# The output product of an attention, SoLU and expert kernel moved one round further behind the hidden product, and the expert slots' row transposes issued ahead of their weight loads

## The chip, the cores and the metric

One core of a Trainium2 chip runs one launch. The metric is device time in microseconds (us); lower is better. The engines are TensorE (PE in the rows; PEld is its weight load), VectorE (DVE), ScalarE (ACT), GpSimd (POOL) and SyncE (SP), which issues most of the transfers. L516 is line 516 of the kernel.

## The reference

The inputs are attention tensors of 8 batches, 8 heads, 576 positions and 64 dimensions, and the weights of two layers behind it.

```python
# 1: attention inside chunks of 64 positions
scores = q_c @ k_c.T / 8;  attn = softmax(scores);  x = attn @ v_c      # -> 4608 tokens x 512
# 2: a SoLU layer
h = x @ w_in                                       # 4608 x 1024
solu = h * softmax(h)
ln = (solu - mean) / sqrt(var + 1e-6) * g_ln
x2 = ln @ w_out                                    # 4608 x 512
# 3: each token goes to the one expert with its largest logit
e = argmax(x2 @ w_gate);  gate = max of softmax(x2 @ w_gate)
out = gate * sigmoid(x2 @ w_output_gate)[e] * (relu(x2 @ w1[e]) @ w2[e])
```

All products run in float16 pairs (a high part and a rest), three matmuls for one.

## The kernel before, in words

**Stage 1** works on 36 tiles of 128 tokens (NT = 36). It is a software pipeline written out by hand: a table of step names, each with an offset. In round i the step `ma+0` handles tile i, `pv+1` tile i+1, and so on; each engine runs its own instructions in exactly this order. START (lines 38 to 47) lists the first rounds one by one, BODY (lines 50 to 53) the rest; the loop at line 825 runs BODY for rounds 4 to 37. The steps that matter here:

- `ma` (m1, L461): the hidden product h of a tile, 24 matmuls of 512 columns on PE into the one pair of PSUM banks of `ps_h`.
- `hm`, `eh`, `um` (L472 to L492): row maximum on DVE (L474), exponential on ACT (L481), their product u on DVE (L488), which is h's last reader. The next `ma` cannot start before it.
- `uh`, `ul`, `ud` (L507 to L522): u is centred and split, its high half on ACT (L510), its rest on DVE (L516), and `ud` has SP transpose both by a DMA (L521) into `uT`, of which there are three buffers.
- `mb` (m2, L524; in the loop through `m2_tile`, L791): the output product x2, 48 matmuls (L534), from `uT` into the one pair of PSUM banks of `ps_x`.
- `ev`, `el` (L540, L553): x2 is read out, on ACT (logits L548, rows L550) and on DVE (L556). The next `mb` cannot start before both.
- `ro`, `rk`, `pa` (L559, L586, L601): tokens are routed in groups of four tiles: `ro` some seven small DVE instructions and a few on POOL, `rk` two small matmuls, `pa` some eight more DVE instructions (L610 to L620). `send` (L770) then scatters a tile's rows to DRAM from POOL (L644).
- `pr`, `pe`, `pv`, `qk` and the steps around them: the attention of tiles one to three ahead. `ya`, `yb`: one expert weight piece is split on ACT (L273) and DVE (L274), in every third round two, until 40 of 64 are done.

Before the change `mb` handles tile i-1 and `ev`, `el`, `ro` tile i-2. The last tile's `m2_tile` puts the first expert slot's first product `ffn1(0)` ahead of m2(35) on PE. At the end of round 33 POOL also gathers the rows of three early slots (L182), which SP transposes in rounds 34 to 36 (L192).

**Stage 2** (from line 854) runs expert slots of 128 tokens. Slot s has on PE `ffn1` (tile hc, 96 matmuls; j = 0, 1) and `ffn2` (tile y, 24 matmuls), one slot after the other. Even slots use weight lane W0, odd ones W1. While slot s runs, SP issues for slot s+2: the first matrix (`wload(s+2, parts=[0])`, L950, two transfers of 1 MB, carried out only where the lane changes its expert), the transpose of the slot's gathered rows (`xtr_slot`, L192), the next weight piece's store and load, and, after `ffn2(s)`, the second matrix. The rows are gathered by POOL (L182) at the end of the slot before.

SP works strictly in order. The program's transfers from SP and ACT take turns on eight completion counters, and one waits until the transfer that had its counter before has landed, whether or not it needs that data. Which transfers fall on one counter follows from the order of the program.

Of the kernel before, what the change touches and what calls it, by code (L numbers as in the profile page):

```python
# [20 lines left out]
NT = NTOK // P  # L21
# [7 lines left out]
GRP = max(GROUPS)  # L29
# [7 lines left out]
FIRST = 4  # L37
# [4 lines left out]
gm1 oh5 tp3 su2 te3 wp0 gm2 no1V tp4 ld6 te4 ex2 gm3 hm0 tp5 pt1 te5 ph1 gm4 qk3 tp6 ol1 te6 ol7 gm5 eh0 tp7 ol6 te7  # L42
pl1 gm6 pv1 gm7 mx3 sm2 no2G xh1 su3 sc4G xl1 um0 ex3 pt2 ol5 oh4 uh0 ma1 hi4 ph2 sq0 sm3 ul0 ol3 sc6G pl2 lo4G ol0
ol4 ol2 pv2 hm1 xh2 ld7 gE0 eh1 no3G xl2 qk4 mb0 mx4 pt3 su4 hi5 sc7A um1 ph3 ss0 ex4 uh1 lo5V qk5 ld8 ev0 pl3 sm4
no4G pv3 ma2 ul1 sq1 mx5 el0 xh3 xl3 su5 hi6 pt4 mb1 lo6G qk6 ex5 ph4 hm2 eh2 pl4 sc8A sm5 um2 ss1 pv4 uh2 ev1 ma3
no5G sq2 xh4 hi7 ul2 mx6 ld9 xl4 pt5 su6 ex6 el1 sm6 mb2 hm3 no6G ph5 eh3 pl5 um3 ss2 sq3 uh3 ul3 lo7G ss3
"""


BODY = """  # L50
ev-2 el-2 pe+1 ph+2 pl+2 ya+0 ys+0 yl+0 ma+0 yb+0 yt+0 ym+0 pv+1 qk+3 hq+4 hk+4 xh+1 lq+4 sA+0 lk+4 sB+0 hm+0
eh+0 xl+1 sc+5 mx+3 um+0 uh+0 su+3 ex+3 sq+0 ul+0 mb-1 sm+3 ud+0 pr+2 rk-3 pa-3 ld+6 no+3 ss+0 ro-2
"""


# [10 lines left out]
def tile_attention_solu_moe(  # L66
# [12 lines left out]
    V, A, G, T, SP = nc.vector, nc.scalar, nc.gpsimd, nc.tensor, nc.sync  # L79
# [14 lines left out]
    spare = const.tile([P, 1], F32, name="spare")  # L94
# [81 lines left out]
    def sync(i, o):  # L176
        tc.add_manual_dep(i.ins, o.ins.name, mybir.DependencyInfo(
            mybir.DependencyClass.Sync, mybir.DependencyReason.DATA), reason="order")

    def gather(s, gx, far, after=()):  # L180
        x = xs[s % NX]
        i = G.indirect_dma_start(out=x.bitcast(I32), out_offset=None, in_=rows,  # L182
                                 in_offset=bass.IndirectOffsetOnAxis(ap=gx, axis=0),
                                 bounds_check=NE * NTOK - 1, oob_is_err=False)
        for o in after:
            sync(i, o)
        cst["x", s] = (x, far)
        cst["g", s] = i

    def xtr(s, xT):  # L190
        x, _ = cst["x", s]
        SP.dma_start_transpose(out=xT.rearrange("p s k t -> p (s k) t"), in_=x[:, 0:DM].bitcast(F16))  # L192
        cst["xT", s] = xT
# [45 lines left out]
    def reach(s):  # L239

        order = range(NE) if s % 2 == 0 else range(NE - 1, -1, -1)
        n = sum(s // 2 >= k for k in FILL[s % 2])
        return set(order) if n == 3 else set(order[:n + 1])
# [43 lines left out]
    with ExitStack() as ab:  # L287
# [225 lines left out]
        def ulo(t):  # L513
            u, se, _ = st["u", t]
            us = st["us", t]
            V.scalar_tensor_tensor(out=us[:, 1], in0=u, scalar=se[:, 2:3], in1=us[:, 0], op0=ALU.add, op1=ALU.subtract)  # L516

        def u_tr(t):
            us = st.pop(("us", t))
            uT = u_p.tile([P, 2, FC, P], F16, tag="uT", name="uT", bufs=3)  # L520
            SP.dma_start_transpose(out=uT.rearrange("p s f t -> p (s f) t"), in_=us.rearrange("p s f -> p (s f)"))  # L521
            st["uT", t] = uT  # L522
# [221 lines left out]
        def consts(_):  # L744
# [8 lines left out]
            ld=load, sc=scale_qv, hi=split_hi, lo=split_lo, qk=qk, mx=smax, su=ssub, ex=sexp, sm=ssum, no=snorm,  # L753
            pt=pt_pe, ph=pt_hi, pl=pt_lo, pv=pv, xh=xt_hi, xl=xt_lo, ma=m1, hm=hmax, eh=exph, um=umul, uh=uhi,
            sq=stats, ul=lambda t: (ulo(t), u_tr(t)), ss=stats2, mb=m2, ev=x2_ev, el=x2_lo,
# [14 lines left out]
        def send():  # L770
            nonlocal sent
            if sent < routed:
                scatter(sent)
                sent += 1
# [39 lines left out]
        def early_pieces(t, n, f):  # L814
            if t < NT - 2 and done[0] < AHEAD and (n == 0 or t % 3 == 1):
                f()

        steps.update(
            ph=p_hi, pl=p_lo, pr=p_tr, pe=pt_ev, ul=ulo, ud=u_tr, hq=qv_hi, hk=k_hi,
            lq=qv_lo, lk=k_lo, mb=m2_tile, rk=rank, pa=place_rows,  # L820
            ro=route_rows, sA=lambda t: ok(t + 4) and send(), sB=lambda t: ok(t + 4) and send(),
            ya=lambda t: early_pieces(t, 0, piece_split), ys=lambda t: early_pieces(t, 0, piece_store),
            yl=lambda t: early_pieces(t, 0, piece_load), yb=lambda t: early_pieces(t, 1, piece_split),
            yt=lambda t: early_pieces(t, 1, piece_store), ym=lambda t: early_pieces(t, 1, piece_load))
        for i in range(FIRST, NT + 2):
            if i - FIRST < NX:
                G.memset(xs[i - FIRST], 0.0)
            for name in BODY.split():
                t = i + int(name[2:])
                if ok(t):  # L830
                    steps[name[:2]](t)
            if not ok(i + 4):
                n = 2 if i < NT else GRP
                while n and sent < routed:
                    send()
                    n -= 1
                    if n:
                        G.memset(spare, 0.0)
            if i == NT - 3:
                raws = [raw_p.tile([P, 3, 512], F32, tag="raw", name=f"raw{j}") for j in range(2)]  # L840
                for j in range(EARLY):
                    gather(j, egx[:, j:j + 1], efar[:, j:j + 1],
                           after=[scattered[t] for t in range(sum(GROUPS[:EG + 1]))])
                    G.memset(spare, 0.0)
            if NT - 2 <= i < NT - 2 + EARLY:
                j = i - (NT - 2)
                xtr(j, raws[0][:, j].bitcast(F16).rearrange("p (s k t) -> p s k t", s=2, k=KC))
            for n in range(2):
                if 0 <= i - (NT - 5) < 4:
                    m, kc = divmod(2 * (i - (NT - 5)) + n, KC)  # L850
                    SP.dma_start(out=W0[m][:, kc], in_=(wsp1, wsp2)[m][0, :, kc])


    with ExitStack() as cs:
# [50 lines left out]
        def new(tag, k):  # L905
            return x_p.tile([P, 2, 4, P], F16, tag=tag, name=tag, bufs=k)
# [30 lines left out]
        def wload(s, e=None, parts=(0, 1)):  # L937
            kw = {}
            if e is None:
                if 0 in parts:  # L940
                    cst["e", s] = (SP.value_load(ei[0:1, s:s + 1], min_val=0, max_val=NE - 1),
                                   SP.value_load(ei[0:1, NS + s:NS + s + 1], min_val=0, max_val=1))
                e, c = cst["e", s]
                kw = dict(cond=(c > 0))
            for m in parts:
                for hk in range(2):
                    kk = slice(2 * hk, 2 * hk + 2)
                    src = (wsp1, wsp2)[m]
                    src = src[e, :, kk] if not kw else src[ds(e, 1), :, kk].rearrange("a p k s f -> (a p) k s f")
                    i = SP.dma_start(out=W[s % 2][m][:, kk], in_=src, **kw)  # L950
                    can = reach(s) if kw else {e}
                    assert not can & {x for _, x, _ in pieces[done[0]:]}, (s, can, done)
                    for o, x in stores:
                        if x not in can:
                            tc.declare_no_dep(i.ins, o.ins, reason="another expert")
                    wloads.append((i, can))
                    if not kw:
                        sync(i, (scattered[-1], cst.get(("g", EARLY + 1)))[m])

        def next_piece():  # L960
            piece_split()
            piece_store()
            piece_load()

        def fetch_slot(k):
            gather(k + EARLY, gx[:, k:k + 1], far[:, k:k + 1], after=scattered if k == 0 else ())

        def xtr_slot(k):
            xtr(k + EARLY, new("xT", 3))

        def ffn(s, w, between=lambda: None):
            ffn1(s, w[0], [new("hT0", 2), new("hT1", 2)])
            between()
            ffn2(s, w[1])
# [15 lines left out]
        def slots(a, b):  # L990
            for s in range(a, b):
                def between():
                    if s + 2 < b:
                        wload(s + 2, parts=[0])
                        xtr_slot(s + 2)
                        next_piece()

                ffn(s + EARLY, W[s % 2], between)
                if s + 2 < b:
                    wload(s + 2, parts=[1])  # L1000
                    if s % 8 == 7:
                        next_piece()
                put(s + EARLY, x_p)
                if s + 3 < b:
                    fetch_slot(s + 3)
                else:
                    G.memset(spare, 0.0)

        slots(0, OFTEN)
        n = nc.values_load(ei[0:1, 2 * NS:2 * NS + 1], min_val=0, max_val=NS)  # L1010
# [63 lines left out]
```

## Time and profile before

| | |
|---|---|
| median of 3 runs | 988.37 us (985.55 to 988.44) |
| the profiled execution | 986.18 us, of which its span is 984.2 us |
| granted TensorE clock, mean | 0.974 |
| stage 1, first to last x2 matmul | 94 to 547 us |
| stage 2, first to last slot | 576 to 979 us |
| DMA, mean over the span | 204 GB/s |

The profile lists for each engine its instructions with start, duration, and the idle time ahead of them with what ended it. A row of the timeline reads: start in us from the span's start, duration in us, engine, line, operation, tile written <- tiles read, shapes, count; in brackets the idle time before it and the releaser. A row of the waits reads: who waited <- for whom: us in total, times, longest. A row of the chain of waits gives start, duration and the piece of work; "DMA" there is the time from issue to landing. Ends of matmuls are modelled, so steps on PE are best read from start to start.

### The profile page before, as it was taken

To read this page: it belongs to the slowest core of one execution; us is meant where nothing else is said; L and a number is where in the kernel's file an instruction comes from. 1 tells how busy PE (TensorE), PEld (TensorE's weight loads), DVE (VectorE), ACT (ScalarE), POOL (GpSimd) and SP (SyncE) were. 2 spreads that over 40 slices of the span, in tenths; PEclk is the share of its full clock that TensorE was granted. 3 is DMA by queue.
4 is the path that set the end of the run, shared out by engine and by line. 5 is a ranking of instruction groups with operands and counts; after the bars stand their busy time and mean duration, and the time that the engine had idled before them with its cause. 6 is when DMAs were issued, how large, how long until landed. Compare 5 with 4: busy or idle time off the path is not lost.

```text
span 984.2 us, 26880 instructions
## 1 busy us (share of the span) xinstructions
PE 897.7 (91%) x11230; PEld 635.1 (65%) x11230; DVE 538.3 (55%) x964; ACT 453.6 (46%) x697; POOL 402.9 (41%) x503
## 2 busy tenths in 40 slices
PE   0378999998999899989999999998999999999996
PEld 0165666666666666656667767775776677777774
DVE  7947679898988888888875613221222222111110
ACT  3435677776777777777663123232222222111111
POOL 4815366767666766666534321121111121121120
PEclk9956999999999999999999999999999999999999
DMA  9432467877786978778678677889799753943252
GB/s 381 144 107 55 106 175 208 241 229 228 230 262 194 276 222 237 234 196 254 183 226 202 167 231 230 269 246 287 204 265 309 231 172 101 339 128 78 65 172 92
DMA packets 161442, 201.18 MB, mean 204 GB/s; under 512 B 123164, under 2 KB 123164, under 8 KB 156192
## 3 DMA queue, kind: packets, MB, share of 16 engines
q1 hardware_dynamic: 148576, 158.39, 56.7%
q0 software_dynamic: 9280, 28.40, 8.5%
q10 hardware_dynamic: 3456, 12.58, 3.5%
q8 instruction: 90, 1.47, 0.6%
q14 instruction: 40, 0.33, 0.1%
HBM read 244.40 MB, written 53.51 MB: 303 GB/s over the span
## 4 chain that ended last, share of the span: by engine, by line
PE 46%; DVE 28%; DMA 8%; issue 8%; ACT 6%; POOL 2%; SPq 2%; DVEq 0%; ACTq 0%; POOLq 0%
PE hc L92 19%; PE y L92 16%; DVE us L516 5%; PE x L534 5%; DVE ws L274 4%; DVE u L488 4%; ACT us L510 3%; DVE mm L474 3%; PE h L92 3%; DMA uT<-us 2%; DMA xT<-xs 2%; DMA w<-wsp 2%; DVE ssum L376 2%; PE gx L736 1%; ACT ws L273 1%
## 5 line engine op out<-in xcount | busy, mean ns | idle before, releaser
L92 PEld LDWEIGHTS <-w 128*128 128x128 f16 x3840 | 220.6, 99 | 17.5 <-issue 7.2
L534 PE MATMUL x<-wo,uT 128*128 128x272 f16 x1728 | 204.3, 279 | 18.9 <-DMA uT<-us 16.2
L206 DVE SCALAR_TENSOR_TENSOR hT<-hc,hT 128x512 f16<-128x512 f32 x78 | 53.9, 691 | 295.5 <-ACT hT L205 289.2
L92 PE MATMUL hc<-xT,w 128*128 128x128 f16 x3552 | 207.7, 220 | 5.0 <-DMA xT<-xs 5.0
L92 PE MATMUL y<-w,hT 128*128 128x512 f16 x936 | 208.9, 379 | 1.7 <-DMA w<-wsp 1.5
L92 PE MATMUL h<-wi,xT 128*128 128x512 f16 x864 | 196.1, 384 | 10.5 <-DVE xT L456 8.6
L534 PEld LDWEIGHTS <-uT 128*128 128x128 f16 x1728 | 167.6, 99 | 48.2 <-DMA uT<-us 18.5
L226 POOL DMA_INDIRECT out_dram<-o,ix x40 | 40.8, 1021 | 326.8 <-ACT o L225 306.8
L92 PEld LDWEIGHTS <-hT 128*128 128x128 f16 x936 | 89.7, 98 | 103.6 <-issue 2.1
L92 PEld LDWEIGHTS <-xT 128*128 128x128 f16 x864 | 83.6, 99 | 107.4 <-DVE xT L456 9.5
L205 ACT ACTIVATE hT<-hc 128x512 f16<-128x512 f32 x78 | 46.6, 597 | 155.5 <-PE hc L92 147.2
L324 POOL TENSOR_TENSOR qv<-raw,qv 128x1024 f16<-128x1024 f32 x35 | 81.3, 2322 | 44.7 <-ACT qv L315 44.7
L225 ACT ACTIVATE o<-y,xs 128x512 f32<-128x512 f32 x40 | 27.5, 688 | 152.2 <-PE y L92 141.5
L274 DVE SCALAR_TENSOR_TENSOR ws<-wf,ws 128x1024 f16<-128x1024 f32 x64 | 79.4, 1253 | 31.6 <-ACT ws L273 31.4
L383 POOL TENSOR_TENSOR p<-p,ssum 128x512 f32<-128x512 f32 x35 | 38.1, 1088 | 134.9 <-DVE ssum L378 71.0
L273 ACT ACTIVATE ws<-wf 128x1024 f16<-128x1024 f32 x64 | 65.9, 1044 | 22.2 <-DMA wf<-in_w_dram 20.6
L516 DVE SCALAR_TENSOR_TENSOR us<-u,se,us 128x1024 f16<-128x1024 f32 x36 | 61.1, 1696 | 23.4 <-ACT us L510 23.2
L510 ACT ACTIVATE us<-u,se 128x1024 f16<-128x1024 f32 x36 | 41.3, 1148 | 49.3 <-DVE se L490 49.3
L481 ACT ACTIVATE e<-h,mm 128x1024 f32<-128x1024 f32 x36 | 40.1, 1114 | 37.5 <-DVE mm L475 37.5
L488 DVE SCALAR_TENSOR_TENSOR u<-h,e 128x1024 f32<-128x1024 f32 x36 | 44.0, 1223 | 7.2 <-ACT e L481 3.2
L474 DVE TENSOR_REDUCE mm<-h 128x1 f32<-128x1024 f32 x36 | 43.8, 1217 | 6.3 <-PE h L92 6.3
L644 POOL DMA_INDIRECT rows<-row,ix x36 | 39.1, 1086 | 16.1 <-DVE row L620 8.0
(183 smaller groups left out, 972.3 us busy)
## 6 DMA issues: line engine op xcount, KB each, us to landing
w<-wsp SPq DMA_DIRECT2D x152, 1024.0 KB
wf<-in_w_dram SPq DMA_DIRECT2D x64, 512.0 KB
raw<-in_qvk_dram SPq DMA_DIRECT2D x36, 768.0 KB
wsp<-ws SPq DMA_DIRECT2D x40, 512.0 KB
wsp<-ws ACTq DMA_DIRECT2D x24, 512.0 KB
w<-in_w_in_dram SPq DMA_DIRECT2D x4, 1024.0 KB
w<-wsp SPq DMA_DIRECT2D x8, 512.0 KB
wo<-in_w_out_dram SPq DMA_DIRECT2D x2, 1024.0 KB
```

The source lines that it names most:

```text
L92: T.matmul(ps, lhsT=l, rhs=r, start=(i == 0), stop=(i == n - 1))
L205: A.activation(t[:, 0], h, AF.Relu)
L206: V.scalar_tensor_tensor(out=t[:, 1], in0=h, scalar=0.0, in1=t[:, 0], op0=ALU.max, op1=ALU.subtract)
L226: i = G.indirect_dma_start(out=out, out_offset=bass.IndirectOffsetOnAxis(ap=ix, axis=0), in_=o, in_offset=None, bounds_check=NTOK - 1, oob ...
L273: A.activation(s16[:, 0], f, AF.Copy, scale=S_E)
L274: V.scalar_tensor_tensor(out=s16[:, 1], in0=f, scalar=S_E, in1=s16[:, 0], op0=ALU.mult, op1=ALU.subtract)
L324: E.tensor_tensor(out=qv[:, 1], in0=raw, in1=qv[:, 0], op=ALU.subtract)
L474: V.tensor_reduce(mm[:, 0:1], h.rearrange("p a b -> p (a b)"), axis=AX.X, op=ALU.max)
L488: V.scalar_tensor_tensor(out=u, in0=h.rearrange("p a b -> p (a b)"), scalar=S_U / (S_X * S_WI), in1=e, op0=ALU.mult, op1=ALU.mult, accum_o ...
L510: A.activation(us[:, 0], u, AF.Identity, bias=se[:, 2:3])
L516: V.scalar_tensor_tensor(out=us[:, 1], in0=u, scalar=se[:, 2:3], in1=us[:, 0], op0=ALU.add, op1=ALU.subtract)
L534: T.matmul(x2[:, z, 0:n], lhsT=uT[:, a, f], rhs=wo[b][:, f, z, 0:n], start=(f + a + b == 0), stop=(last and a + b == 0))
```

## The change

The three later steps (`ev`, `el`, `mb`) and the routing that follows are moved one round further back: `mb` from tile i-1 to i-2, `ev`, `el` and `ro` from i-2 to i-3, `rk` and `pa` from i-3 to i-4. START gives up one `mb`, one `ev` and one `el`; the loop gets one more round, 38. The scatters at the end have a small POOL memset behind each instead of between them, and the round from which four may be sent is one later. In stage 2 the transpose of slot s+2 is issued ahead of the first matrix of slot s+2 instead of behind it.

```diff
-no4G pv3 ma2 ul1 sq1 mx5 el0 ... sc8A sm5 um2 ss1 pv4 uh2 ev1 ma3
-no5G sq2 xh4 hi7 ul2 mx6 ld9 xl4 pt5 su6 ex6 el1 sm6 mb2 hm3 no6G ...
+no4G pv3 ma2 ul1 sq1 mx5 el0 ... sc8A sm5 um2 ss1 pv4 uh2 ma3
+no5G sq2 xh4 hi7 ul2 mx6 ld9 xl4 pt5 su6 ex6 sm6 hm3 no6G ...
 BODY = """
-ev-2 el-2 pe+1 ph+2 pl+2 ya+0 ys+0 yl+0 ma+0 ...
-eh+0 xl+1 sc+5 ... ul+0 mb-1 sm+3 ud+0 pr+2 rk-3 pa-3 ld+6 no+3 ss+0 ro-2
+ev-3 el-3 pe+1 ph+2 pl+2 ya+0 ys+0 yl+0 ma+0 ...
+eh+0 xl+1 sc+5 ... ul+0 mb-2 sm+3 ud+0 pr+2 rk-4 pa-4 ld+6 no+3 ss+0 ro-3
...
-        for i in range(FIRST, NT + 2):
+        for i in range(FIRST, NT + 3):
...
-                n = 2 if i < NT else GRP
+                n = 2 if i <= NT else GRP
                 while n and sent < routed:
                     send()
                     n -= 1
-                    if n:
-                        G.memset(spare, 0.0)
+                    G.memset(spare, 0.0)
...
                     if s + 2 < b:
+                        xtr_slot(s + 2)
                         wload(s + 2, parts=[0])
-                        xtr_slot(s + 2)
                         next_piece()
```

## Rows read from the trace of the kernel before

**Rows 1.** The profile's busy time, share of the span and instructions of each engine:

```profile
PE 897.7 (91%) x11230; PEld 635.1 (65%) x11230; DVE 538.3 (55%) x964; ACT 453.6 (46%) x697; POOL 402.9 (41%) x503
```

**Rows 2.** Waits of the whole execution: PE for the transposed u, and in stage 2:

```profile
PE x L534 <- DMA uT<-us: 16.2, 14, 3.0
...
PE hc L92 <- DMA xT<-xs: 5.0, 2, 4.1
```

**Rows 3.** Waits of DVE alone, 127 to 512 us:

```profile
DVE us L516 <- ACT us L510: 19.8, 31, 2.4
...
DVE mm L474 <- PE h L92: 0.8, 2, 0.4
```

**Rows 4.** Timeline, DVE: the row maximum of tile 6 and of tile 32:

```profile
157.31 1.21 DVE L474 TENSOR_REDUCE mm<-h 128x1 f32<-128x1024 f32 x1
...
494.67 1.22 DVE L474 TENSOR_REDUCE mm<-h 128x1 f32<-128x1024 f32 x1
```

**Rows 5.** Timeline, PE: h of two tiles, with no wait between them:

```profile
139.74 5.34 PE L92 MATMUL h<-wi,xT 128*128 128x512 f16 x24
...
151.80 5.34 PE L92 MATMUL h<-wi,xT 128*128 128x512 f16 x24
```

**Rows 6.** Timeline, PE: end of stage 1, h of tiles 33 to 35 and what follows:

```profile
499.88 5.34 PE L92 MATMUL h<-wi,xT 128*128 128x512 f16 x24
...
512.10 5.34 PE L92 MATMUL h<-wi,xT 128*128 128x512 f16 x24
...
524.75 5.34 PE L92 MATMUL h<-wi,xT 128*128 128x512 f16 x24
530.38 5.57 PE L534 MATMUL x<-wo,uT 128*128 128x272 f16 x48 [0.29 <-DMA uT<-us]
535.79 4.68 PE L92 MATMUL hc<-raw,w 128*128 128x128 f16 x81
...
541.72 4.89 PE L534 MATMUL x<-wo,uT 128*128 128x272 f16 x42
...
547.17 5.34 PE L92 MATMUL y<-w,raw 128*128 128x512 f16 x24
```

**Rows 7.** Timeline, DVE, end of stage 1: u of tile 32, the last rounds' chain, the readout:

```profile
497.40 1.23 DVE L488 SCALAR_TENSOR_TENSOR u<-h,e 128x1024 f32<-128x1024 f32 x1
...
525.87 0.18 DVE L610 TENSOR_TENSOR rw<-rt,eoff 128x32 f32<-128x32 f32 x1
...
527.20 0.72 DVE L556 SCALAR_TENSOR_TENSOR row<-x,se,row 128x512 f16<-128x512 f32 x1
...
530.13 1.23 DVE L474 TENSOR_REDUCE mm<-h 128x1 f32<-128x1024 f32 x1 [2.21 <-PE h L92]
...
535.53 1.28 DVE L516 SCALAR_TENSOR_TENSOR us<-u,se,us 128x1024 f16<-128x1024 f32 x1 [1.16 <-ACT us L510]
...
548.38 0.75 DVE L556 SCALAR_TENSOR_TENSOR row<-x,se,row 128x512 f16<-128x512 f32 x1 [0.28 <-ACT row L550]
```

**Rows 8.** Timeline, PE, stage 2: the two slots that waited for their rows:

```profile
685.58 8.32 PE L92 MATMUL hc<-xT,w 128*128 128x128 f16 x96 [4.13 <-DMA xT<-xs]
...
765.43 5.52 PE L92 MATMUL hc<-xT,w 128*128 128x128 f16 x96 [0.92 <-DMA xT<-xs]
```

**Rows 9.** Waits of PE, 545 us to the end: for weights:

```profile
PE y L92 <- DMA w<-wsp: 1.5, 2, 0.8
```

**Rows 10.** Waits of SP's queue, 600 to 690 us:

```profile
SPq L192 <- DMA wsp<-ws: 24.2, 3, 10.7
```

**Rows 11.** Timeline, SP: a slot's transpose, and the weight loads behind it:

```profile
666.01 1.33 SPq L192 DMA_TRANSPOSE xT<-xs  x1
...
668.34 1.08 SPq L950 DMA_DIRECT2D w<-wsp  x2
```

**Rows 12.** The chain of waits, 440 to 700 us, issue to landing:

```profile
489.71 4.27 DMA uT<-us
...
672.20 13.24 DMA xT<-xs
```

More of the change, by code (lines that the diff above doesn't have):

```diff
@@ L44 @@
 ol4 ol2 pv2 hm1 xh2 ld7 gE0 eh1 no3G xl2 qk4 mb0 mx4 pt3 su4 hi5 sc7A um1 ph3 ss0 ex4 uh1 lo5V qk5 ld8 ev0 pl3 sm4
-no4G pv3 ma2 ul1 sq1 mx5 el0 xh3 xl3 su5 hi6 pt4 mb1 lo6G qk6 ex5 ph4 hm2 eh2 pl4 sc8A sm5 um2 ss1 pv4 uh2 ev1 ma3
-no5G sq2 xh4 hi7 ul2 mx6 ld9 xl4 pt5 su6 ex6 el1 sm6 mb2 hm3 no6G ph5 eh3 pl5 um3 ss2 sq3 uh3 ul3 lo7G ss3
+no4G pv3 ma2 ul1 sq1 mx5 el0 xh3 xl3 su5 hi6 pt4 mb1 lo6G qk6 ex5 ph4 hm2 eh2 pl4 sc8A sm5 um2 ss1 pv4 uh2 ma3
+no5G sq2 xh4 hi7 ul2 mx6 ld9 xl4 pt5 su6 ex6 sm6 hm3 no6G ph5 eh3 pl5 um3 ss2 sq3 uh3 ul3 lo7G ss3
 """
 BODY = """
-ev-2 el-2 pe+1 ph+2 pl+2 ya+0 ys+0 yl+0 ma+0 yb+0 yt+0 ym+0 pv+1 qk+3 hq+4 hk+4 xh+1 lq+4 sA+0 lk+4 sB+0 hm+0
-eh+0 xl+1 sc+5 mx+3 um+0 uh+0 su+3 ex+3 sq+0 ul+0 mb-1 sm+3 ud+0 pr+2 rk-3 pa-3 ld+6 no+3 ss+0 ro-2
+ev-3 el-3 pe+1 ph+2 pl+2 ya+0 ys+0 yl+0 ma+0 yb+0 yt+0 ym+0 pv+1 qk+3 hq+4 hk+4 xh+1 lq+4 sA+0 lk+4 sB+0 hm+0
+eh+0 xl+1 sc+5 mx+3 um+0 uh+0 su+3 ex+3 sq+0 ul+0 mb-2 sm+3 ud+0 pr+2 rk-4 pa-4 ld+6 no+3 ss+0 ro-3
 """
```

## The prediction, made before the changed kernel was run

> **What bounds the kernel now.** I read the page's busy line first: PE is busy 91% of the span, DVE 55% [rows 1]. Then the waits: PE waits 16.2 us in 14 places for the transposed u, the operand of m2 [rows 2]. Those two together suggest that PE is the bound and that the change, which gives the transposition of u one more round to arrive, is worth some 16 us. The next view speaks against that. The share of busy time is a mean over stages, and in stage 1 the question is who waits last. Between 127 and 512 us DVE waits for PE only 0.8 us, in 2 places, though each of its rounds begins with a row maximum of what PE has just made; what it does wait for is ACT, for the high half of u, 19.8 us in 31 places [rows 3]. The row maxima of tiles 6 and 32 stand at 157.31 and 494.67 [rows 4]: (494.67 - 157.31) / 26 = 12.98 us a round. PE, where it waits for nothing, makes its round in 151.80 - 139.74 = 12.06 us [rows 5]. So DVE with its link to ACT sets the round, and PE has 12.98 - 12.06 = 0.92 us in each to wait somewhere. It now waits ahead of m2 for u's transposition. Behind that wait stands the next `ma`, which needs DVE's last reader of h. If the wait at m2 goes, PE stands at `ma` instead, for u of L488.
>
> **Steady rounds.** mb-2 takes away the wait for a transposition that takes 4.27 us from issue to landing on the chain of waits [rows 12]. A round more covers it three times. DVE's, ACT's and POOL's instructions stay the same in number; ev and el read a tile one round older, and stand at the same place of their queues, at the head of a round, ahead of `pe`. Their m2 was then done even longer ago, so they add no wait. Gain: none if DVE is never late through PE; at most 0.8 us, all that DVE waits for PE [rows 3]. I take 0. START gives up one m2, ev and el; the step that they leave is DVE's as well, so 0 there, and the work comes back in the drain.
>
> **The drain.** The last rounds have less attention in them, DVE has less to do, and PE becomes the bound: the steps of `ma` are 12.22 and 12.65 us for tiles 33 and 34 [rows 6], and DVE waits 2.21 us for h of tile 35 [rows 7]. There a round that is one longer in depth costs time. Step by step:
> 1. u of tile 32 ends at 497.40 + 1.23 = 498.63 [rows 7], m1(33) begins at 499.88 [rows 6]. With m2 no longer late, m1(33) can begin at 498.63: 1.25 earlier. Round 33 keeps its 12.22: m1(34) at 510.85. Round 34 loses about 1.0 of its 12.65, which by estimate is the part above the others' step and belongs to the same lateness: m1(35) at 522.5, or 2.25 before today's 524.75.
> 2. m2(33) follows m1(35) after 530.38 - 524.75 - 0.29 = 5.34 us, so at 527.84, and lasts 535.79 - 530.38 = 5.41 [rows 6], to 533.25.
> 3. m2(34) now comes with no m1 between. It needs both banks of `ps_x` read out. Today ev and el of a tile always run beside an m1. DVE's order in round 36 is: ul(35), a routing step `pa`, then el(33) at the head of the next pass. The row maximum of tile 35 ends 5.38 after m1(35) starts, 530.13 - 524.75 [rows 6, 7], so begins at 527.88; from it to the end of ul are 535.53 + 1.28 - 530.13 = 6.68, so 534.56; the routing runs 527.20 - 525.87 = 1.33, el 0.72 [rows 7]: 536.61. m2(34) begins at about 536.65, 3.4 us after the one before it.
> 4. m2(34) 5.41, the early slot's first product 541.72 - 535.79 = 5.93, m2(35) 547.17 - 541.72 = 5.45 [rows 6]: the first y begins at 553.45, today at 547.17. Cost **6.3 us**.
> Bounds: if m2(34) waits only for a bare readout, as the last tile's today, from 547.17 to 548.38 + 0.75 [rows 6, 7], 2.0 us, rather than for the DVE queue ahead of it, the cost is 6.3 - 1.4 = 4.9; if m1(35) begins no earlier than today, 6.3 + 2.25 = 8.5. I take 6.3, since it is read from the order of DVE.
>
> **What else moves.** Scatters go one round later, with one memset more each on POOL, which is 403 us busy of 984 [rows 1] and has nothing urgent behind it there: 0. The early slots' gathers at the end of round 33 now stand directly behind the last two scatters before them; SP's three transposes of these rows are issued in rounds 34 to 36 and wanted only by the early slot's first product, which itself starts some 6 us later: 0, at worst the 2.0 of a readout, which the range takes in. The m2 of the drain needs three live transposed u at most, as many as there are buffers: 0.
>
> **Stage 2.** PE waits here 5.0 us for transposed rows, in 2 places [rows 2]: 4.13 and 0.92 [rows 8]. The first also has a slow product behind it, 8.32 instead of 5.52: 4.13 + 2.80 = 6.93 us for that slot. The rows tell why. SP held three transposes for 24.2 us in all, the longest 10.7, for a weight piece's store, which they don't read: it had the completion counter they are to use [rows 10]. Behind the held one, issued at 666.01, came the second matrix of the same slot at 668.34 [rows 11], and behind that the next slot's transpose, issued at 672.20 and landed 13.24 us later [rows 12], beside or behind 1 MB transfers. With the transpose ahead of the lane's loads the counters shift by the two loads; I expect that the hold falls on something that nobody needs as early, that the loads then go about 1.4 us earlier (the issue of a transpose is 1.33, [rows 11]), and that they have less of a transposition ahead of them, about half of the 4.27 of [rows 12], by estimate 2.1, since a slot's is half as wide. Of the wait 4.13 - 1.4 - 2.1 = 0.6 is left, and the slow product, which a wait of 0.92 did not bring on [rows 8], is gone: 6.93 - 0.6 = 6.3. The other wait for rows gives 0.9, and of the 1.5 us for y's weights [rows 9] the one wait that goes by the same cause gives 0.7. Gain **7.9 us**; bounds 0 (the transfers ahead of the late transpose are the same) and 6.93 + 0.92 + 0.7 = 8.5.
>
> A rule of the Trainium skill speaks against this. In "DMA: Bandwidth & Descriptors", section "Queues, rings and completion order", it says that an SDMA engine consumes the descriptors of a ring in the order in which they stand there, and that SP has one row of rings. By it, the transpose of the late slot still waits for every second-matrix transfer ahead of it, whoever was issued a few instructions earlier, and the sum would be that of the second rival below. That the transpose landed 13.24 us after its issue [rows 12] agrees.
>
> **Sum.** 0 + 6.3 - 7.9 = -1.6. The profiled execution took 986.18 us (span 984.2), 2.2 below the median of 988.37; the mean of it and the three runs is 987.1. I add the change to that mean: **985.5 us**. By the profiled execution alone it would be 984.6.
>
> **Rivals.**
> *PE is the bound after all.* The 16.2 us of [rows 2] come back. The drain's cost is then only that of the lost cover, about 3.4: 987.1 - 16.2 + 3.4 - 7.9 = 966.4. Against it is [rows 3]: DVE all but never waits for PE. Chance 0.06.
> *Slower: the late transpose stays late.* Place: SP's queue in stage 2, where the transpose of the slot after a change of expert stands behind the second matrix. If the order within the slot doesn't matter, stage 2 gives 0 to 1.6 (the other waits), and the drain costs 6.3: 987.1 + 4.7 to 987.1 + 6.3, 991.8 to 993.4. It decides as soon as the gain in stage 2 is under 6.3 - 3.0 = 3.3. For it: the 13.24 of [rows 12]; against it: the 10.7 us hold [rows 10], which put the matrix where it is and is what the change touches. Chance 0.22.
> *The drain costs little.* The readout of tile 33 is ready sooner, for instance because the row maximum of tile 35 and all behind it on DVE come earlier than [rows 7] say; m1(35) gains its 2.25 and m2(34) waits 1 rather than 3.4. Cost 2 to 4, net -4 to -6: about 982. Chance 0.18.
> *The change in stage 2 does nothing that it says,* as the counters fall so that another transfer holds SP as long, and the drain is as today, too: 987. Chance 0.04.
> My forecast has the rest, 0.50, with a range of its own of 981 to 990.
>
> **Numbers.** A measurement of this kernel tells about 0.3% from no change, 3.0 us: faster is below 984.1, slower above 990.1. Of the forecast's 0.50 about 0.18 are below, 0.27 within and 0.05 above; the first and the third rival give 0.22 to faster, 0.02 to same; the second 0.22 to slower; the last 0.04 to same. Together 0.40, 0.33 and 0.27. The range from 978 to 994 takes in the second rival and the third, and leaves out the first and the far ends.
>
> **What would show it.** PE's wait for the transposed u gone from the list of waits and in its place, as large, one of the hidden product for DVE's u; the row maxima still 12.9 to 13.0 us apart. If they come below 12.7, DVE was not the bound. In the drain, a gap of some 3 us ahead of m2(34), ended by L556 of DVE, and the first y at about 553. In stage 2, no wait for rows over 1 us and no first product over 5.6 us; SP's wait of L192 for the store gone. A late transpose after slot 9's loads, as before, makes the second rival right.

## The result, and the profile after

The changed kernel took 989.13 us in the median of 12 runs, the kernel before 986.49 in 12 beside it: a ratio of 1.0051, 95% interval 1.0029 to 1.0072. Measured once more (a2_again, below) it came to 1.0064 (1.0040 to 1.0088). The medians lie 2.6 us apart and the means of the twelve 4.3; by the ratio, by which all runs are told here, the change is slower by about 5 us. Forecast were 1.6 us less. The execution profiled has a span of 988.3 us, against 984.2.

The profile's busy line, against [rows 1], shows next to nothing:

```profile
PE 900.0 (91%) x11230; PEld 633.8 (64%) x11230; DVE 536.0 (54%) x964; ACT 453.2 (46%) x697; POOL 403.2 (41%) x508
```

**Steady rounds.** PE's waits between 127 and 512 us, before and then after:

```profile
PE x L534 <- DMA uT<-us: 15.8, 12, 3.0
PE rt L594 <- DVE p L364: 1.5, 3, 0.9
PE h L92 <- DVE u L488: 1.4, 1, 1.4
```

```profile
PE h L92 <- DVE u L488: 7.5, 10, 1.3
PE rt L594 <- DVE p L364: 5.3, 6, 1.7
PE x L534 <- DVE row L556: 3.0, 7, 0.4
```

DVE's row maxima of tiles 6 and 32 in the timeline, as in [rows 4]:

```profile
156.45 1.23 DVE L474 TENSOR_REDUCE mm<-h 128x1 f32<-128x1024 f32 x1 [0.29 <-PE h L92]
...
491.92 1.22 DVE L474 TENSOR_REDUCE mm<-h 128x1 f32<-128x1024 f32 x1
```

The wait for the transposed u is gone from this stretch. In its place PE waits 7.5 + 5.3 + 3.0 = 15.8 us for DVE, in all three, where it had waited 1.5 + 1.4 = 2.9. The rounds are (491.92 - 156.45) / 26 = 12.90 us long, against 12.98. That mean hides where the difference lies. The row maxima of tiles 9 and 28, before and then after:

```profile
196.18 1.22 DVE L474 TENSOR_REDUCE mm<-h 128x1 f32<-128x1024 f32 x1
...
441.05 1.22 DVE L474 TENSOR_REDUCE mm<-h 128x1 f32<-128x1024 f32 x1
```

```profile
194.59 1.22 DVE L474 TENSOR_REDUCE mm<-h 128x1 f32<-128x1024 f32 x1
...
439.43 1.22 DVE L474 TENSOR_REDUCE mm<-h 128x1 f32<-128x1024 f32 x1
```

They are 244.87 and 244.84 us apart, 12.89 a round in both: here nothing was won. The 1.9 us that the 26 rounds became shorter are 0.7 between tiles 6 and 9 and 1.2 between tiles 30 and 32.

**The drain.** The timeline of PE at the end of stage 1, against [rows 6]: h of tile 35, then m2(33), m2(34), the early slot's first product, m2(35) and the first y.

```profile
519.59 5.34 PE L92 MATMUL h<-wi,xT 128*128 128x512 f16 x24
524.77 5.56 PE L534 MATMUL x<-wo,uT 128*128 128x272 f16 x48
...
533.67 8.28 PE L534 MATMUL x<-wo,uT 128*128 128x272 f16 x48 [3.30 <-DVE row L556]
541.79 5.52 PE L92 MATMUL hc<-raw,w 128*128 128x128 f16 x96
547.15 4.89 PE L534 MATMUL x<-wo,uT 128*128 128x272 f16 x42
...
552.60 5.34 PE L92 MATMUL y<-w,raw 128*128 128x512 f16 x24
```

And a table by stretches (busy time and count of PE, PEld, DVE, ACT and POOL, then the granted clock, the DMA share and GB/s): the gap, m2(34) and what follows it.

```profile
530.30:533.60 3.30, 0.07 (x3) 0.00 (x0) 3.05 (x10) 2.12 (x7) 1.08 (x3) 0.82 0.59 196
533.70:541.70 8.00, 8.00 (x48) 5.96 (x48) 0.00 (x0) 0.00 (x0) 4.15 (x9) 0.65 1.15 206
541.80:547.00 5.20, 5.20 (x96) 5.20 (x94) 2.61 (x9) 1.45 (x3) 0.59 (x3) 1.00 0.16 57
```

m2(34) waits 3.30 us for the readout of tile 33 by DVE's L556, where 3.4 were forecast. Behind the gap it takes 541.79 - 533.67 = 8.12 us rather than 5.4, at a granted clock of 0.65: partly at 1.2 GHz, after PE had stood still. The first y starts at 552.60, 5.43 us later than at 547.17.

**Stage 2.** From the first y to the end of the span are 988.3 - 552.60 = 435.7 us; before, 984.2 - 547.17 = 437.0. Of the 7.9 us forecast 1.3 came in this pair of profiles (more pairs below). PE's waits from 576 us on:

```profile
PE y L92 <- ACT hT L205: 2.7, 2, 2.1
PE hc L92 <- DMA xT<-xs: 2.3, 2, 1.4
PE hc L92 <- DMA w<-wsp: 1.3, 2, 0.7
PE y L92 <- DMA w<-wsp: 0.5, 1, 0.5
```

The late slot of [rows 8] doesn't wait here, but others do. Two kinds of wait are not in the profile of before: the first product (hc) for its matrix, and the second (y) for ACT's hT. The latter is in a second profile of the kernel before (b2_again, below), with 1.27 and 0.70 us, so it doesn't come of the change; the former, beyond slot 0, is in no profile with the old order. SP's waits from 576 to 970 us, before and then after:

```profile
SPq L192 <- DMA wsp<-ws: 64.5, 9, 11.9
...
SPq L950 <- DMA wsp<-ws: 19.7, 4, 6.5
SPq L192 <- DMA xs<-rows,c: 18.1, 13, 5.8
```

```profile
SPq L192 <- DMA xs<-rows,c: 123.2, 31, 9.2
SPq L949 <- DMA wsp<-ws: 23.5, 12, 4.3
```

The hold of the transposes for a weight store went, as forecast. But the transpose now comes so early that SP stands at it for the gather of the rows, in 31 places, with the matrices and the weight piece behind it in SP's order. PE's waits at slots 9, 17 and 26, and one of ACT:

```profile
678.99 5.20 PE L92 MATMUL hc<-xT,w 128*128 128x128 f16 x90 [0.62 <-DMA w<-wsp]
...
772.96 5.65 PE L92 MATMUL y<-w,hT 128*128 128x512 f16 x24 [2.07 <-ACT hT L205]
...
864.00 5.20 PE L92 MATMUL hc<-xT,w 128*128 128x128 f16 x90 [0.65 <-DMA w<-wsp]
```

```profile
768.91 1.06 ACT L273 ACTIVATE ws<-wf 128x1024 f16<-128x1024 f32 x1 [8.93 <-DMA wf<-in_w_dram]
```

ACT stands 8.93 us at the split of a weight piece that has not arrived, and the eviction of hT is behind it in ACT's order. It stands so in the kernel before, too: in 4 places in either, the longest 7.7 us there and 10.2 in its second profile.

### The profile page after: what moved, and what is told of

Same layout as the page of the kernel before. It is cut to its first block, busy times and chain, and to the rows that moved or that the text cites. A ratio compares the mean times of both kernels' runs of the same rounds, so it can differ in the third digit from the quotient of the medians.

```text
span 988.3 us, 26863 instructions
## 1 busy us (share of the span) xinstructions
PE 900.0 (91%) x11230; PEld 633.8 (64%) x11230; DVE 536.0 (54%) x964; ACT 453.2 (46%) x697; POOL 403.2 (41%) x508
## 4 chain that ended last, share of the span: by engine, by line
PE 50%; DVE 27%; DMA 8%; issue 7%; ACT 6%; POOL 2%; SPq 0%; ACTq 0%; POOLq 0%; DVEq 0%
PE hc L92 18%; PE y L92 16%; PE h L92 7%; PE x L534 5%; DVE us L516 4%; DVE ws L274 4%; DVE u L488 4%; DVE mm L474 3%; DMA xT<-xs 3%; ACT us L510 2%; DMA wf<-in_w_dram 2%; ACT ws L273 2%; DVE ssum L376 1%; PE gx L736 1%; POOL p L383 1%
## 5 line engine op out<-in xcount | busy, mean ns | idle before, releaser
L92 PEld LDWEIGHTS <-w 128*128 128x128 f16 x3840 | 217.6, 98 | 16.2 <-issue 6.0
L92 PE MATMUL h<-wi,xT 128*128 128x512 f16 x864 | 199.9, 389 | 20.4 <-DVE u L488 11.2
L92 PE MATMUL hc<-xT,w 128*128 128x128 f16 x3552 | 205.1, 219 | 3.7 <-DMA xT<-xs 2.3
L274 DVE SCALAR_TENSOR_TENSOR ws<-wf,ws 128x1024 f16<-128x1024 f32 x64 | 77.4, 1223 | 34.1 <-ACT ws L273 34.0
```

What stands on the lines that cost most here:

```text
L92: T.matmul(ps, lhsT=l, rhs=r, start=(i == 0), stop=(i == n - 1))
L274: V.scalar_tensor_tensor(out=s16[:, 1], in0=f, scalar=S_E, in1=s16[:, 0], op0=ALU.mult, op1=ALU.subtract)
```

## The experiments

Times are ratios to the kernel before in the same set of runs on the same chip (its medians there were 981.7 to 984.5). Slots are counted from 0 for the first that is transposed into `xT`.

**The two parts alone.** First the lag with the old order on SP, then the swap on the kernel before.

```diff
 # e1_lag_only, against the changed kernel
-                        xtr_slot(s + 2)
                         wload(s + 2, parts=[0])
+                        xtr_slot(s + 2)
 # e2_swap_only, against the kernel before: the reverse
```

> Only the stage-1 part of the change: x2 two rounds behind h; in stage 2 the old order, a slot's transpose behind its first matrix. My theory: the drain's bare m2(34) is what the lag costs, the steady stretch gives back 2 to 4 us before it, so the first y begins 5 to 6 us later than in the kernel before (552 to 553 against 547.17), and stage 2 lasts from there as long as before, 437 +- 2 us: 4 to 7 us slower than before, gap of 3.3 us ahead of m2(34) ended by L556 and that m2 some 8.3 long. Rival (the loss comes from the order on SP in stage 2, the lag is free): first y within 1 us of 547, time within 2 us of before.

> Only the stage-2 part: the kernel before, with a slot's transpose issued ahead of its first matrix. My theory: SP now stands at the transpose until the slot's gather has landed (its wait of L192 for the gathered rows goes from 27 us in 15 places to over 100 us in some 30), with the matrices and the weight piece behind it; the 4.13 and the slow product of one slot go, but waits for weights and for the hidden product's eviction of the experts come, so stage 2 takes 435 +- 2.5 against 437 us and the time is between -3 and +1 us of before. Rival (stage 2 gives back nothing and costs on its own): +3 us or more. Rival of the prediction on record: -8 us, no wait for rows over 1 us left.

The lag alone came to 1.0061 (1.0033 to 1.0089), 6 us, within the 4 to 7 expected, so the drain's loss is the lag's own. From the first y on it took 433.1 us, less than the 437 +- 2 expected. m2(34) has the same gap and the same slow run, and the first y starts at 553.34:

```profile
534.27 8.43 PE L534 MATMUL x<-wo,uT 128*128 128x272 f16 x48 [3.30 <-DVE row L556]
...
553.34 5.34 PE L92 MATMUL y<-w,raw 128*128 128x512 f16 x24
```

The swap alone came to 1.0050 (1.0023 to 1.0077): outside the first theory's -3 to +1 us, as its rival said (+3 or more), and far from the prediction's -8. The execution profiled is the fastest of the twelve, 979.92 us, so its waits tell where time goes, not how much. SP's waits from 576 us, SP's transpose for slot 10, and PE's first products of slots 10, 17 and 26 in the timeline:

```profile
SPq L192 <- DMA xs<-rows,c: 132.5, 32, 9.3
```

```profile
667.32 3.50 SPq L192 DMA_TRANSPOSE xT<-xs  x1
```

```profile
680.96 5.52 PE L92 MATMUL hc<-xT,w 128*128 128x128 f16 x96 [2.80 <-DMA xT<-xs]
...
757.34 7.15 PE L92 MATMUL hc<-xT,w 128*128 128x128 f16 x96 [2.23 <-DMA xT<-xs]
...
854.89 5.20 PE L92 MATMUL hc<-xT,w 128*128 128x128 f16 x90 [0.57 <-DMA w<-wsp]
```

So the waits for rows that the swap was to end are still there, at the same slots, and a wait for a first matrix is added. From the issue of slot 10's transpose to its product are 680.96 - 667.32 = 13.64 us; before, 685.58 - 672.20 = 13.38 [rows 8, 12]. The transpose comes no sooner for standing ahead of its slot's first matrix. Both parts cost, each by itself.

**The drain covered.** The early slot's first product goes ahead of m2(34) and half of its second product ahead of m2(35); once with the swap, once without.

```diff
...
+            if t == NT - 2:
+                ffn1(0, ...)
             if t != NT - 1:
                 m2(t)
                 return
             route(ends[t - 1])
-            ffn1(0, ...)
+            ffn2(0, W0[1], range(0, FC // 2))
...
-                ffn2(0, W0[1])
+                ffn2(0, W0[1], range(FC // 2, FC))
```

> The changed kernel, with the bare spot of its drain covered: the early slot's first product stands ahead of m2(34) instead of ahead of m2(35), and half of that slot's second product stands between m2(34) and m2(35). My theory: the 3.30 us wait of m2(34) and its 2.7 us of slow running both go, nothing takes their place, so the time is 5 to 6 us under the changed kernel's, 1 to 2 under the kernel before. Rival (the wait goes elsewhere: evictions of the expert's product delay the readout of x2 on ACT and DVE): 0 to 3 us under the changed kernel.

> The lag of the change and the covered drain, with the old order in stage 2. My theory: first y as early as 546 to 547.5 or earlier, stage 2 as before, 437 +- 2: within 2 us of the kernel before, 0.5 to 2 us slower than the run with the covered drain and the new order. Rival (the old order is the better one): 1 us or more faster than that run.

PE's timeline of e3_covered has no gap and no slow m2, m2(34) at 535.33, but a new wait of 2.08 us at the last tile's ranks, for POOL:

```profile
529.97 5.52 PE L92 MATMUL hc<-raw,w 128*128 128x128 f16 x96
535.33 5.56 PE L535 MATMUL x<-wo,uT 128*128 128x272 f16 x48
540.73 2.75 PE L218 MATMUL y<-w,raw 128*128 128x512 f16 x12
...
553.92 0.17 PE L596 MATMUL rt<-oh,ones 128*128 128x8 f16 x1 [2.08 <-POOL oh L581]
```

Both theories expected too much. With the swap the time is 1.0059 (1.0034 to 1.0085), no better than the changed kernel's 1.0051 and 1.0064, as the rival said (0 to 3 us, the wait goes elsewhere, here to POOL). Without it, it is 1.0034 (1.0010 to 1.0059), against 1.0061 of the lag alone: 3.3 us above the kernel before where at most 2 were expected, and by its rival some 2.5 below the run with the swap, with intervals that overlap. Slot 0 starts 4.7 us earlier than in the lag's own run (576.52 against 581.26), and half of that, 2.7 us, is seen in the time, with intervals that overlap.

**Once more, and the gathers earlier.** The changed kernel and the kernel before again, for second profiles; the changed kernel with each gather issued a slot earlier; and, as a pair without the lag, swap and old order both with the earlier gathers.

```diff
         put(2, x_p)
+        fetch_slot(3)
...
-                if s + 3 < b:
-                    fetch_slot(s + 3)
+                if s + 4 < b:
+                    fetch_slot(s + 4)
```

> The changed kernel once more, so that it is measured on one chip with the runs beside it and has a second profile. The lag alone cost 0.6% and the swap alone 0.5%. Theory one (each has its own place, so they add): 8 to 11 us slower than before. Theory two (stage 2 waits for transfers that keep their own pace, so part of what stage 1 loses is given back there): 4 to 7 us slower, as in its first measurement. In its stage 2 I expect, by either, waits at other slots than in the first profile but again at the slots about 10, 17 and 27.

> The kernel before once more, for a second profile of it. Whether the 4.13 us wait of one slot for its rows, with 2.8 us of slow running behind it, is the kernel's or that execution's: if the kernel's, the same slot waits 3.5 us or more again; if that execution's, another amount, under 3 us.

> The changed kernel with each slot's gather one slot earlier (one gather more ahead of the loop, then the gather of s+4 instead of s+3 behind the stores of slot s); the order on SP stays that of the change. My theory: what the swap costs is that SP stands at the transpose for the gather with the matrices and the weight piece behind it. With the gather earlier its waits of L192 for gathered rows fall from 131 us to under 40, the waits of PE for weights and for the evictions of hT go, and the time is 3 to 6 us under the changed kernel's. Rival (SP's standing there costs nothing, transfers set the pace): within 2 us of the changed kernel.

> The kernel before with the swap alone and each slot's gather one slot earlier, so that SP no longer stands at the transposes for the gathers. The swap alone cost 0.50% [0.23, 0.77]. Theory one (SP's standing with the loads behind it is what the swap costs): no wait of PE for a first matrix but the first slot's, and the time within 0.15% of the kernel beside it, which has the early gathers and the old order. Theory two (a transposition ahead of the loads costs by itself, or the bursts decide): 0.3% or more above that kernel.

> The kernel before with the earlier gathers and the old order: the control of the run beside it. SP waits little for gathers here already (18 us in 13 places), so by either theory within 0.2% of the kernel before; the transposes about slots 10 and 17 still stand behind the matrices of the slot before and PE still waits 1.5 to 4 us there.

The changed kernel again gave 1.0064, in theory two's range, though by their intervals the parts (0.61% and 0.50%) may also add. Its PE waits about slots 10, 17 and 27 again, and at slot 5. In the second profile of the kernel before the slot that had cost 4.13 + 2.80 us waits 2.31 and has no slow product, so the size was that execution's:

```profile
682.91 5.52 PE L92 MATMUL hc<-xT,w 128*128 128x128 f16 x96 [2.31 <-DMA xT<-xs]
```

In the control with earlier gathers and the old order the same slot waits 5.00 us and is slow again, 7.88:

```profile
686.68 7.88 PE L92 MATMUL hc<-xT,w 128*128 128x128 f16 x96 [5.00 <-DMA xT<-xs]
```

The earlier gathers ended SP's wait for them (in e5_gather_early nothing of it is left among the larger ones), and PE's waits for the first matrices of slots 9 and 26 with it (only slot 0's is left, 1.22 us). Slots 5, 10 and 17 wait for their rows, 3.21, 2.02 and 1.17 us, and SP now stands at the matrices for the weight pieces' stores, 83.1 us, about as long as it did before the change at transposes and matrices together, 64.5 + 19.7:

```profile
SPq L949 <- DMA wsp<-ws: 83.1, 19, 8.4
```

```profile
635.68 7.15 PE L92 MATMUL hc<-xT,w 128*128 128x128 f16 x96 [3.21 <-DMA xT<-xs]
```

The time is 1.0053 (1.0033 to 1.0074): my theory of 3 to 6 us fell, the rival held. In the pair, the swap has 1.0025 (1.0001 to 1.0049) and the old order 0.9996 (0.9977 to 1.0015). So the swap's 0.50% falls to about 0.29% once SP needn't wait for gathers, with intervals that overlap on every side. That SP's standing for gathers makes first matrices late is shown; that it costs time is not, and what the swap's cost consists of stays open.

**Transposes ahead of both matrices.** On the kernel before, slot s issues the transpose of slot s+3, ahead of its loads for s+2, with gathers two slots earlier and a fourth `xT`.

```diff
...
+                    if s + 3 < b:
+                        xtr_slot(s + 3)
                     if s + 2 < b:
                         wload(s + 2, parts=[0])
-                        xtr_slot(s + 2)
                         next_piece()
...
-                if s + 3 < b:
-                    fetch_slot(s + 3)
+                if s + 5 < b:
+                    fetch_slot(s + 5)
```

> The kernel before, with the transpose of slot s+3 (instead of s+2) issued in slot s, ahead of the loads for slot s+2, and the gathers two slots earlier; four buffers for the transposed rows. So a slot's transpose stands ahead of both matrices of the slot before it as well, which the change's swap does not reach. My theory: the late transposes of the slots about 10 and 17 (4.1 and 0.9 us in the profile of before, 1.5 to 2.9 in the others, with either order) come from standing behind those matrices in SP's queue; now no wait for transposed rows over 0.3 us is left, and the time is 3 to 7 us under the kernel before. Rival (the transfers are late as a whole, so the wait only turns into one for the weights): within 2 us of before.

0.9978 (0.9957 to 0.9999): 2.2 us faster, less than the 3 to 7 expected, though the waits for rows went as the theory had it. PE's waits from 576 us have one row left (slot 0, ahead of that, waits 1.49 us for its first matrix, as in most of these runs):

```profile
PE y L92 <- ACT hT L205: 3.9, 1, 3.9
```

No transpose is late for PE any more, and earlier gathers alone, in the control above, didn't do it. By the events on the trace's completion counters slot 10's transpose, issued at 647.71 ahead of both matrices of slot 9, lands 6.5 us later, where it took 13.24 [rows 12]. Slot 11's, which now stands behind those two matrices, is issued at 661.73 and takes 14.9 us, but it is wanted a slot later. So a transpose behind the matrices of the slot before is late, and the swap leaves it there. This run gives it another place and a slot more of time at once and doesn't separate the two. The one wait that is left is ACT's, for a weight piece.

**Is DVE the bound?** In each round of stage 1 DVE's half of a weight piece (L274) moves to where DVE waits for ACT ahead of u's rest; ACT's half stays, the piece's store and load follow DVE's half, and the second piece of every third round goes to the head. With the lag (old order in stage 2), and with x2 one round behind h.

```diff
-... ya+0 ys+0 yl+0 ma+0 yb+0 yt+0 ym+0 pv+1 ...
+... yb+0 yt+0 ym+0 ma+0 ya+0 pv+1 ...
-... um+0 uh+0 su+3 ex+3 sq+0 ul+0 mb-2 ...
+... um+0 uh+0 su+3 yz+0 ex+3 sq+0 ul+0 ys+0 yl+0 mb-2 ...
 # ya: ACT's half of the piece alone (L273); yz: DVE's half
```

> The lag of the change with the old order in stage 2, and DVE's round made shorter in each round of stage 1: of the one weight piece of every round, ACT's half stays where it was and DVE's half (L274, 1.22 us) stands between u and its rest, where DVE waits for ACT 0.56 us a round (us L516 <- ACT us L510). My theory: DVE's ring sets the round, so each of some 28 rounds gets 0.5 us shorter, from 12.90 to about 12.4, and the time is 10 to 15 us under the run with the lag alone. Rival (PE or another link sets it): 12.8 or more a round, within 3 us of the lag alone.

> The same edit on the kernel before, with x2 one round behind h. My theory: u's rest and its transposition come later, and m2, one round behind, waits longer for them, so that little of the shorter DVE ring is left: 12.7 to 12.95 a round, 0 to 6 us under the kernel before. Then the lag is worth something only where DVE's ring is shorter than PE's path through the transposition. Rival (the transposition has slack of its own here): 12.4 a round as with the lag, 10 us or more under before, and the lag is worth nothing either way.

With the lag, 0.9920 (0.9895 to 0.9945); without it, 1.0075 (1.0047 to 1.0102). The row maxima of tiles 6 and 32, first with the lag, then without:

```profile
155.08 1.22 DVE L481 TENSOR_REDUCE mm<-h 128x1 f32<-128x1024 f32 x1 [1.29 <-PE h L92]
...
476.17 1.22 DVE L481 TENSOR_REDUCE mm<-h 128x1 f32<-128x1024 f32 x1
```

```profile
157.62 1.22 DVE L481 TENSOR_REDUCE mm<-h 128x1 f32<-128x1024 f32 x1 [0.62 <-PE h L92]
...
498.09 1.23 DVE L481 TENSOR_REDUCE mm<-h 128x1 f32<-128x1024 f32 x1 [1.60 <-PE h L92]
```

That is 321.09 / 26 = 12.35 us a round against 340.47 / 26 = 13.10. In the second, PE waits for the transposed u and DVE for PE's h (waits of each, 127 to 500 us):

```profile
PE x L541 <- DMA uT<-us: 19.2, 16, 2.8
```

```profile
DVE mm L481 <- PE h L92: 23.5, 21, 2.6
```

DVE's own work, from one row maximum to the next, did set the round of the changed kernel: made shorter, the round follows, as expected, and the lag alone's 1.0061 becomes 0.9920, 1.4% less. With x2 one round behind, the same edit delays u's rest and so its transposition, and by the waits the loop through it becomes the bound; that it would cost some 7 us by the ratio (5.8 by the medians), not give 0 to 6, I had not expected. Between the two the lag is worth about 1.5%.

**All together:** lag, covered drain, DVE filled, far transposes.

> Lag, covered drain, DVE's round filled, the transposes of s+3 ahead of the loads for s+2 with gathers two slots earlier. If the parts add: lag with covered drain +3, the DVE filling -12, the far transposes -2.4: about 11 us under the kernel before. If stage 2 takes back what comes earlier, because its transfers keep their own pace: 3 to 7 us under.

0.9877 (0.9853 to 0.9902), 969.18 against 981.71 us: 12 us faster than the kernel before, about the sum of the parts, and the fastest of the study.

## Why the prediction was right, and where it failed

**Steady rounds: right.** Forecast were 0, with PE's wait moved to DVE's u. The wait moved (15.8 us, in three places, only 7.5 of it to u), and from tile 9 to tile 28 the round stayed at 12.89 us. What was won, 1.9 us, lies at the two ends of the stretch, above the bound of 0.8: most of it in the step from tile 30 to 31, 16.22 us before and 13.52 after, of which the next gives 1.48 back. Why was not tested. DVE as the bound is shown by the pair with the filled DVE, and the rival "PE is the bound" falls by it.

**The drain: right in size, by luck, as two terms offset.** 6.3 us were forecast up to the first y; the two profiles' are 5.43 apart. One pair is one draw of what varies between executions, so take all profiles: slot 0 starts at 575.68, 574.87, 571.58, 571.61, 574.83 and 575.77 us with x2 one round behind (mean 574.1), and at 581.22, 578.90, 581.26 and 579.45 with the bare lag (mean 580.2), 6.1 later. (The two runs with the covered drain and those with the filled DVE are not among these.) The mechanism is as told: m2(34) with no m1 between, 3.30 us of wait for 3.4, ended by L556. Missing in the sum were the 8.12 - 5.41 = 2.7 us that m2(34) loses at the lower clock behind its gap (8.26 in the lag's own run, 6.95 in the two other profiles with it). From m1(35) to the first y the same profiles with the lag take 10.4 us longer in the mean, not 8.5. Against that, m1(35) began 524.75 - 519.59 = 5.2 us earlier, not 2.25; in the mean of the same profiles 4.1. How far one profile may be off, e6_transpose_far shows: with the same stage 1 as the kernel before, it has its first y at 543.40, 3.8 us sooner.

**Stage 2: this step failed.** That of 6.93 us at one slot 6.3 would come back, and 7.9 with the smaller waits, was wrong on three counts; the failure was in the mechanism as well as in the size.
- *The size was one execution's.* With the old order that slot waited 4.13 us in the profile that I had, and 2.31, 2.61, 1.51, 3.44, 2.38 and 5.00 in six others (mean of all 3.1). With the swap it waits 0 to 2.87 in six (mean 1.7), but other slots wait more: for rows at all slots together PE waits 3.7 us in the mean of the seven, and 4.7 in that of the six. From slot 0 to the last y the old order takes 395.69, 394.38, 392.30, 389.43, 394.69, 389.39 and 396.56 us in seven profiles (mean 393.2), the swap 394.81, 398.01, 393.75, 396.85, 396.60 and 394.21 in six (mean 395.7). The two spreads overlap, but a gain of 7.9 is nowhere in them: the swap costs some 2.5 us.
- *The transpose was not freed.* It still landed late behind the matrices of the slot before: 13.64 us from issue to product in the run with the swap alone, 13.38 before. e6_transpose_far puts it ahead of those, a slot earlier, and the waits for rows end. That was the second rival ("the late transpose stays late", 991.8 to 993.4), with 0.22. By the measured ratio the mean of 987.1 becomes 987.1 x 1.0051 = 992.1. The rule of the Trainium skill ("DMA: Bandwidth & Descriptors", section "Queues, rings and completion order") that a ring's descriptors are consumed in their order pointed to it; the far transposes agree, with 6.5 us to landing ahead of the matrices and 14.9 behind them.
- *A wait was overlooked.* I costed what the transposes no longer stand behind, and not what then stands behind them. SP waits 123.2 us for gathers in 31 places in place of 18.1 in 13, and the matrices and the weight piece are queued behind. The order of the program would have told it: the gather is issued only at the end of the slot before. What this wait costs is not shown: with earlier gathers the changed kernel has 1.0053 rather than 1.0064.

**The sum.** -1.6 was 0 + 6.3 - 7.9. By the profiles it is 6.1 up to slot 0 (the steady rounds' gain in it) and 2.5 behind it, 8.6; by the times 5 to 6. Why the parts give less together stays open; the intervals of the parts don't exclude a plain sum (0.33 + 0.23 = 0.56%). START, costed at 0, cost nothing in the mean: from the row maximum of tile 2 to that of tile 6 are 48.11 to 48.14 us in six profiles with x2 one round behind, and 47.48 to 48.98 in six with the lag (mean 48.2).

## What to carry to other kernels

A stall that hangs on a burst of transfers has a place in the kernel, but its size in one profile is a draw: price it by the mean of several executions, or keep the whole of it in the range. A transfer moved ahead in a queue brings its own wait with it, so ask what it waits for at the new place and what is queued behind. More depth in a pipeline pays only where the wait that it removes is the longest loop (here it was worth nothing until DVE's work in a round was made shorter; then the lag was worth some 15 us against the same edit without it, and the two together 8 against the kernel before), and its price is in the drain, where the work that used to cover a readout has run out.

## What the runs showed of the hardware

How long PE stands still does not alone decide whether its clock falls. Behind 3.30 us of wait m2(34) had a granted clock of 0.65 and took 2.7 us longer. In the run with the swap alone the first product behind 2.80 us of wait ran in 5.52 us, that behind 2.23 us in 7.15. The stretches of these last two products, columns as above:

```profile
681.00:686.20 5.20, 5.20 (x94) 5.20 (x95) 0.69 (x1) 0.60 (x1) 2.04 (x2) 1.00 1.06 343
757.40:764.30 6.90, 6.90 (x96) 6.90 (x97) 1.66 (x3) 2.23 (x3) 0.61 (x1) 0.75 0.84 248
```

So a wait of 2 to 3 us may cost another 7.15 - 5.52 = 1.6 us behind it, or nothing. Behind the same wait of 3.3 us m2(34) lasted 8.28 and 8.43 us in two profiles with the lag, 7.11 and 7.12 in two others.

Executions of one program differ here by more than 1%: the kernel before took 976.82 to 989.73 us in 35 runs on one chip. In six profiles with its stage 1 the rounds from tile 9 to tile 28 repeat to a few hundredths, but for one round, which took 12.38 us in four, 12.50 in one and 15.08 in one. What else differs lies ahead of tile 2, in the last rounds of stage 1, and in the stage with the weight transfers.
